# Routing the third batch one step sooner and reordering gathers and stores in a fused attention and mixture-of-experts kernel

## The chip, the cores and the metric

The kernel runs on one core of one Trainium2 chip. A core has five engines that run side by side: TensorE (PE in the profile: matmuls, with PEld for its weight loads), VectorE (DVE), ScalarE (ACT), GpSimd (POOL) and SyncE (SP). Each engine works through a queue of its own, in order, and waits on semaphores for what the others and the transfers produce. The metric is the device time of one execution in microseconds (us), the median of several runs. Lower is better.

## The reference

Two blocks follow one another. The first is a linear attention over 4 batches, 4 heads, 1088 positions and 32 channels, whose features are products of two random sketches. The second sends each of the resulting 4352 tokens of 128 channels to one of 8 experts.

```python
def phi(x):
    a = np.einsum('rd,bhsd->bhsr', S1, x)          # r = 8
    b = np.einsum('rd,bhsd->bhsr', S2, x)
    return np.einsum('bhsi,bhsj->bhsij', a, b).reshape(*x.shape[:-1], r * r)
q_p, k_p = (phi(q), phi(k))
kv = np.einsum('bhsf,bhsd->bhfd', k_p, v)
z = np.sum(k_p, axis=2)
num = np.einsum('bhsf,bhfd->bhsd', q_p, kv)
den = np.einsum('bhsf,bhf->bhs', q_p, z)[..., None] + 1e-06
attn_out = (num / den).astype(np.float32)

x = attn_out.transpose(0, 2, 1, 3).reshape(B * S, H * D)      # 4352 x 128
logits = x @ w_gate                                           # 8 experts
expert_idx = np.argmax(logits, axis=1)
gate_w = softmax(logits)[np.arange(N), expert_idx]            # (written out in the reference)
for e in range(E):
    mask = expert_idx == e
    h = np.maximum(x[mask] @ w1[e], 0.0)                      # 128 -> 1024
    out[mask] = gate_w[mask, None] * (h @ w2[e])              # 1024 -> 128
```

## The kernel before

The attention part is written as steps; the functions put at a step run in the order of a small number given with them. Tokens come out of it batch by batch. `route` handles one batch in four parts: `choose` (the best expert, on DVE), `gates` (the exponential, on ACT), `rank` (a row number for each token, from counting matmuls on PE and seven DVE operations), and `scatter` (POOL writes each group of 128 rows into an array in HBM that is sorted by expert, with one indirect DMA each).

```python
def rank():
    ...
    nc.vector.tensor_reduce(row_i, rk, AX.X, ALU.add)
    nc.vector.tensor_tensor(base_e, base_e, pr[:, ts(n, E)], ALU.add)
    ...
def scatter(us):
    for u in us:
        d = nc.gpsimd.indirect_dma_start(
            out=xs_dram[:], out_offset=bass.IndirectOffsetOnAxis(ap=row_i[:, u:u + 1], axis=0),
            in_=x[:, u, :].bitcast(I32), ...)
```

The sorted rows are then worked on in tiles of 128 rows with a single expert each. Between 34 and 41 tiles are needed, depending on how the tokens fall: tiles 0 to 33 always run (JMIN = 34, JT = 41). Tiles 34 to 40 are optional, in three parts of 4, 2 and 1 tiles, run after tiles 16, 20 and 24 if a bit of a count is set. The first ten tiles (JE = 10) hold only rows of the first two batches, so they can start while batches 3 and 4 are still being routed. For every tile, POOL gathers its rows from HBM; `x_in` transposes them on PE and copies the expert's first weights on DVE; `up` and `down` are the two matmul layers; `store` scatters the rows of the result to `out`, again with an indirect DMA of POOL.

```python
parts = [range(JMIN, JMIN + 4), range(JMIN + 4, JMIN + 6), range(JMIN + 6, JMIN + 7)]
after = {16: 0, 20: 1, 24: 2}
sequence = []
for j in range(JMIN):
    sequence += [j, *parts[after[j]]] if j in after else [j]
place = {j: p for p, j in enumerate(sequence)}
...
def gather(j):
    d = nc.gpsimd.indirect_dma_start(out=xg_bufs[place[j] % XB].bitcast(I32), ..., in_=xs_dram[:], ...)
...
def x_in(j):
    xg = xg_bufs[place[j] % XB]
    xTp = bank_ps(f"xgTp{j}")
    nc.tensor.transpose(xTp[:, :128], in_=xg[:, 0:DM], identity=ident)
    ...
def down(j):
    ...
    nc.scalar.activation(y, py[:, :DM], AF.Copy, bias=0.0, scale=xg_bufs[place[j] % XB][:, DM:DM + 1])
```

The schedule of the third batch (number 2), and the loop over the tiles:

```python
query_chunk(16, 3, 0)
query_chunk(17, 3, 1, turned=(19, 7))      # the transposes of this chunk: step 19, order 7
...
at(16, first_gathers, 0)                   # gathers of tiles 0 to 5
choose, gates, rank, scatter = route(None, 2, J)
at(18, choose, 2)
at(19, gates, 5)
at(20, rank, 6)
at(20, lambda: scatter(range(J)), 6)
at(20, lambda: x_in(0), 0)
at(20, lambda: x_in(1), 5)
at(21, lambda: up(0), 0)
...
def gather_to(p):
    nonlocal gathered
    while gathered < min(p, JT):
        gather(sequence[gathered])
        gathered += 1
...                                        # extras: the fourth batch's routing, in tiles 0 to 5
for j in range(JMIN):
    ...                                    # x_in(j + 2), up(j + 1), extras, down(j); the optional parts
    gather_to(JE if j < 5 else place[min(j + AHEAD, JMIN - 1)] + 1)      # AHEAD = 6

    if j >= 5:
        for _ in range(min(len(waiting), 2 if j + 1 < JMIN else JT)):
            store(waiting.pop(0))
```

`waiting` lists the tiles whose results are computed but not yet stored. Gathers go in the order in which tiles run, with the four optional tiles of the first part between 16 and 17, into 14 buffers in turn. Results of tiles 0 to 33 have 16 buffers in turn (`y`), those of optional tiles one each (`y_late`).

Of the kernel before, what the change touches and what calls it, by code (L numbers as in the profile page):

```python
# [35 lines left out]
I32 = mybir.dt.int32  # L36
AF = mybir.ActivationFunctionType
# [8 lines left out]
def kernel(  # L46
# [12 lines left out]
    nc = tc.nc  # L59
    B, H, S, D = q.shape  # L60
    R = S1.shape[0]
    NTOK, DM = out.shape
    E, _, F = moe_w1.shape
    NP = H // 2
    J = S // 128
# [11 lines left out]
    JT = NTOK // 128 + E - 1  # L77
    JMIN = NTOK // 128

    JE = -(-(NTOK // 2 - E * 127) // 128)  # L80
    XB = 14
    AHEAD = 6
    assert DM == H * D == 128 and H == JC == 4 and R == 8 and REM == 64 and J % JC == 0 and B % 2 == 0
    assert F == 1024 and NTOK == B * S and NTOK % 128 == 0 and E == 8
# [16 lines left out]
    def bank_ps(name):  # L101
        return ps_w.tile([128, 512], FP, tag="w", name=name)
# [108 lines left out]


    xg_bufs = []
    for i in range(XB):
        xg_bufs.append(big.tile([128, XW], FP, name=f"xg{i}"))
        nc.gpsimd.memset(xg_bufs[i], 0.0)

# [71 lines left out]
    def at(step, fn, order=1):  # L289
        steps.setdefault(step, []).append((order, len(steps.get(step, ())), fn))  # L290
# [152 lines left out]
    def rows_of(b, j, n):  # L443
        x, lgh = x_tile(b)
        return x[:, ds(j, n), 0:DM], lgh[:, ds(j, n)]

    def query_chunk(step, b, c, turned=None):
        query(f"{b}_{c}", step,
              [main["q", b][:, h, ts(c, JC), :].rearrange("p j d -> p (j d)") for h in range(H)],
              b, lambda: rows_of(b, c * JC, JC), None, turned or (step + 3, 1))  # L450
# [6 lines left out]
    xs_dram = dram.tile([E * NTOK, XW], I32, name="xs_dram")  # L457
# [193 lines left out]

    parts = [range(JMIN, JMIN + 4), range(JMIN + 4, JMIN + 6), range(JMIN + 6, JMIN + 7)]
    after = {16: 0, 20: 1, 24: 2}
    sequence = []
    for j in range(JMIN):
        sequence += [j, *parts[after[j]]] if j in after else [j]
    place = {j: p for p, j in enumerate(sequence)}
    engines = [PE, DVE, mybir.EngineType.Activation]


    def buffers(name, n, shape, dtype=FP, tags=None):
        def one(k, i):
            if tags is None:
                return big.tile(shape, dtype, name=f"{name}{k}_{i}")
            tag, bufs = tags[k]
            t = io.tile([128, H, J, DA if tag == "v_aug" else D], dtype, tag=tag, name=f"{name}{k}_{i}", bufs=bufs)
            return t.rearrange("p h j d -> p (h j d)")[:, 0:F]

        own = {}

        def of(j):
            k = int(j >= JMIN)
            if k not in own:
                own[k] = [one(k, i) for i in range(n[k])]
            return own[k][j % n[k]]

        return of

    xT_of = buffers("xgT", (3, 2), [128, 128])
    w1_of = buffers("w1", (3, 2), None, tags=(("k", 3), ("q", 3)))  # L680
    hT_of = buffers("hT", (3, 2), None, tags=(("v", 3), ("v_aug", 2)))
# [3 lines left out]
    def y_of(j):  # L685
        if j >= JMIN:
            return late_y[j - JMIN]
        if not early_y:
            for i in range(2):
                t = att.tile([128, JC * H, RR], FP, tag="q_p", name=f"y{i}").rearrange("p g f -> p (g f)")  # L690
                early_y.extend(t[:, ts(c, DM)] for c in range(8))
        return early_y[j % 16]

    def gather(j):
        d = nc.gpsimd.indirect_dma_start(  # L695
            out=xg_bufs[place[j] % XB].bitcast(I32), out_offset=None, in_=xs_dram[:],
            in_offset=bass.IndirectOffsetOnAxis(ap=tiles[j][1], axis=0),
            bounds_check=E * NTOK - 1, oob_is_err=False)
        if j < JE:
            tc.declare_no_dep(d.ins, group="late", reason="late rows are in no tile of the first group")  # L700
            tc.add_to_no_dep_group("early", d.ins)

    def x_in(j):
        xg = xg_bufs[place[j] % XB]
        xTp = bank_ps(f"xgTp{j}")
        nc.tensor.transpose(xTp[:, :128], in_=xg[:, 0:DM], identity=ident)  # L706
        xT, w1 = xT_of(j), w1_of(j)
        nc.scalar.copy(out=xT, in_=xTp[:, :128])  # L708
        _, (wo,) = nc.values_load_multi_w_load_instructions(
            tiles[j][0], engines=[DVE], min_val=0, max_val=(E - 1) * F,  # L710
            skip_runtime_bounds_check_because="the table clamps the expert to the last one")
        nc.vector.tensor_copy(out=w1, in_=w1_all[:, ds(wo, F)])  # L712

    def rows_out(j):

        to = to_of(j)
        row_id = xg_bufs[place[j] % XB][:, DM + 1:DM + 2].bitcast(I32)
        if j < JE:
            nc.vector.tensor_copy(out=to, in_=row_id)
        else:  # L720
            nc.vector.tensor_tensor(to, row_id, tiles[j][2], ALU.bitwise_or)
# [14 lines left out]
    def down(j):  # L736
        hT = hT_of(j)
        _, (wo,) = nc.values_load_multi_w_load_instructions(
            tiles[j][0], engines=[PE], min_val=0, max_val=(E - 1) * F,
            skip_runtime_bounds_check_because="the table clamps the expert to the last one")  # L740
        py = bank_ps(f"py{j}")
        for c in range(NFC):
            nc.tensor.matmul(py[:, :DM], lhsT=hT[:, ts(c, 128)], rhs=w2_all[:, ds(wo + c * DM, DM)],  # L743
                             start=(c == 0), stop=(c == NFC - 1))
        y = y_of(j)
        nc.scalar.activation(y, py[:, :DM], AF.Copy, bias=0.0, scale=xg_bufs[place[j] % XB][:, DM:DM + 1])  # L746

    def store(j):
        y = y_of(j)
# [13 lines left out]
    def run(last):  # L763
        for i in sorted(steps):
            if i <= last:
                for _, _, fn in sorted(steps.pop(i), key=lambda f: f[:2]):
                    fn()

    def first_gathers():
        for j in range(AHEAD):  # L770
            gather(j)
# [33 lines left out]
    key_end(17, 3)  # L805
    query_rem(15, 1)
    query_chunk(16, 3, 0)
    query_chunk(17, 3, 1, turned=(19, 7))
    first_table = table(0, JE, 0)
    for i in range(4):  # L810
        at(14 + i // 2, lambda: next(first_table, None), 4)
# [1 line left out]
    at(16, first_gathers, 0)  # L813
    at(18, lambda: next(first_table, None), 5)
    choose, gates, rank, scatter = route(None, 2, J)
    at(18, choose, 2)
    at(19, gates, 5)
    at(20, rank, 6)
    at(20, lambda: scatter(range(J)), 6)
    at(20, lambda: x_in(0), 0)  # L820
    at(20, lambda: x_in(1), 5)
    at(21, lambda: up(0), 0)
    run(21)

    last_table = table(1, JT - JE, JE)
# [2 lines left out]
        for _ in last_table:  # L830
            break

    gathered = AHEAD

    def gather_to(p):
        nonlocal gathered
        while gathered < min(p, JT):
            gather(sequence[gathered])
            gathered += 1

    choose, gates, rank, scatter = route(None, B - 1, J + 1)
    extras = {0: [choose, gates], 1: [rank, lambda: scatter(range(0, 2))], 2: [lambda: scatter(range(2, 5)), piece],
              3: [lambda: scatter(range(5, 7)), piece, piece], 4: [lambda: scatter(range(7, J + 1)), piece, piece, piece],
              5: [piece, piece, piece]}

    waiting = []
    for j in range(JMIN):
        here = after.get(j)
        if j + 4 == min(after):
            runs = []  # L850
            for i in range(len(parts)):
                _, (v,) = nc.values_load_multi_w_load_instructions(
                    tiles["parts"][0:1, i:i + 1], engines=engines, min_val=0, max_val=E - 1,
                    skip_runtime_bounds_check_because="bits of a number below E")
                runs.append(v)
        if here is not None:
            tiles_here = parts[here]
            rows_out(j)
            for o in tiles_here:
                rows_out(o)  # L860
            with tc.If(runs[here] > 0) as found:
                for i, o in enumerate(tiles_here):
                    if i + 1 < len(tiles_here):
                        x_in(tiles_here[i + 1])
                    else:
                        x_in(j + 2)
                    up(o)
                    down(tiles_here[i - 1] if i else j)
                up(j + 1)
                down(tiles_here[-1])  # L870
            with found.Else():
                x_in(j + 2)
                up(j + 1)
                down(j)
            waiting += [j, *tiles_here]
        else:
            if j + 2 < JMIN:
                x_in(j + 2)
            if j + 1 in after:
                x_in(parts[after[j + 1]][0])  # L880
            rows_out(j)
            if j + 1 < JMIN:
                up(j + 1)
            for fn in extras.get(j, ()):
                fn()
            down(j)
            waiting.append(j)

        gather_to(JE if j < 5 else place[min(j + AHEAD, JMIN - 1)] + 1)

        if j >= 5:
            for _ in range(min(len(waiting), 2 if j + 1 < JMIN else JT)):
                store(waiting.pop(0))


# [29 lines left out]
```

## Time and profile before

| | |
|---|---|
| time, median of 3 runs | 232.16 us (230.89 to 232.24) |
| span of the profiled execution | 230.5 us |
| PE busy | 213.0 us, 92% |
| DVE busy | 115.4 us, 50% |
| ACT busy | 76.7 us, 33% |
| POOL busy | 136.6 us, 59% |
| gathers (xg) | 41 on POOL, 1121 ns each, 2.6 us from issue to landing |
| scatters of rows (xs_dram) | 34 on POOL, 1029 ns each, 2.4 us to landing |
| stores (out_dram) | 34 and 7 on POOL, the 34 at 1047 ns each, 2.3 us to landing |

Times of one execution count from the start of the span. Every group of instructions is told with its engine, its source line (L706 is line 706), what it writes and reads, how often it ran, and the idle time of its engine just before, with what ended it. For the indirect DMAs on POOL the duration is that of the instruction; when the data has landed is told separately. L706 is the transpose in `x_in`, L727 and L743 are the matmuls of `up` and `down`, L519 the scatter of routed rows, L695 the gather, L746 the result (y) and L750 its store.

### The profile page before, as it was taken

The numbers are of one execution on the slowest core, as the hardware profiler recorded it, in microseconds if no ns is written. First come the engines' busy times: TensorE is split into PE (matmuls) and PEld (weight loads), VectorE is DVE, ScalarE is ACT, GpSimd is POOL, SyncE is SP. The second block draws the span as 40 slices with busy tenths as digits, with TensorE's granted clock in tenths as the row PEclk, the third lists the DMA queues.
The fourth block names the chain that finished last, engine by engine and source line by source line (L and its number), as shares of the span: only waits on it lengthen the run. The fifth ranks groups of instructions, "written<-read, shape, count | busy, mean of one in ns | idle before, by whom it ended". The sixth has DMA issues, their size and how long they took to land.

```text
span 230.5 us, 5436 instructions
## 1 busy us (share of the span) xinstructions
PE 213.0 (92%) x1858; PEld 208.7 (91%) x1858; DVE 115.4 (50%) x339; ACT 76.7 (33%) x206; POOL 136.6 (59%) x178
## 2 busy tenths in 40 slices
PE   8799999999996999999499995899999999999992
PEld 8699999999884999999499995899999999999992
DVE  5447478987878688852224243043532433243320
ACT  2424535434434234343113331122322333222230
POOL 3365001277758377776677777777777871762313
PEclk9999999999999999999889999799999999999999
DMA  5899999981111111111011211111111110110000
GB/s 178 192 324 352 342 332 355 340 273 47 49 46 38 35 40 57 46 49 58 25 43 49 57 41 32 40 49 50 47 32 44 50 41 27 33 40 20 14 23 15
DMA packets 22988, 22.61 MB, mean 98 GB/s; under 512 B 5828, under 2 KB 20168, under 8 KB 22960
## 3 DMA queue, kind: packets, MB, share of 16 engines
q1 hardware_dynamic: 19232, 15.08, 22.0%
q0 software_dynamic: 3712, 7.15, 10.5%
q8 instruction: 18, 0.29, 0.5%
q14 instruction: 10, 0.08, 0.1%
q10 hardware_dynamic: 16, 0.00, 0.0%
HBM read 17.81 MB, written 4.95 MB: 99 GB/s over the span
## 4 chain that ended last, share of the span: by engine, by line
PE 67%; issue 10%; DMA 7%; POOL 6%; DVE 4%; ACT 3%; POOLq 1%; DVEq 0%; ACTq 0%
PE ph L727 21%; PE py L743 19%; PE kv L330 7%; PE nd L410 5%; DMA xg<-xs_dram,grow 5%; POOL xs_dram L519 4%; PE ab_q L308 3%; PE ab_k L308 3%; PE qp L395 2%; PE idle L151 2%; DMA xs_dram<-x_rows,row_i 2%; PE xgTp L706 2%; ACT q_pT L398 1%; POOL out_dram L750 1%; PE tp_k L301 1%
## 5 line engine op out<-in xcount | busy, mean ns | idle before, releaser
L727 PE MATMUL ph<-xgT,w 128*128 128x128 f32 x592 | 75.2, 283 | 0.0
L743 PE MATMUL py<-w_all,hT 128*128 x592 | 72.2, 276 | 0.2 <-issue 0.2
L727 PEld LDWEIGHTS ph<-xgT,w 128*128 128x128 f32 x592 | 71.9, 199 | 0.0
L743 PEld LDWEIGHTS py<-w_all,hT 128*128 128x128 f32 x592 | 69.1, 192 | 0.4 <-issue 0.4
L734 DVE TENSOR_SCALAR hT<-ph 128x512 f32<-128x512 f32 x30 | 20.8, 692 | 80.0 <-ACT hT L729 80.0
L695 POOL DMA_INDIRECT xg<-xs_dram,grow x41 | 46.0, 1121 | 16.3 <-issue 9.2
L750 POOL DMA_INDIRECT out_dram<-y,to x34 | 35.6, 1047 | 28.2 <-ACT xgT L708 11.6
L519 POOL DMA_INDIRECT xs_dram<-x_rows,row_i x34 | 35.0, 1029 | 18.4 <-issue 8.8
L729 ACT ACTIVATE hT<-ph 128x512 f32<-128x512 f32 x37 | 22.1, 597 | 55.5 <-PE ph L727 54.1
L712 DVE COPY w<-w_all 128x1024 f32 x38 | 26.2, 695 | 3.8 <-issue 2.1
L746 ACT ACTIVATE y<-py,xg 128x128 f32<-128x128 f32 x34 | 12.5, 367 | 36.2 <-PE py L743 35.1
L410 PE MATMUL nd<-kvx,q_pT 128*128 128x82 f32 x128 | 15.8, 276 | 1.9 <-ACT q_pT L398 1.9
L410 PEld LDWEIGHTS nd<-kvx,q_pT 128*128 128x128 f32 x128 | 14.9, 192 | 2.6 <-ACT q_pT L398 2.6
L182 POOL COPY v_aug<-v 128x1024 f32<-128x1024 f32 x4 | 4.2, 1042 | 20.8 <-DMA v<-in_v_dram 20.8
L706 PE MATMUL xgTp<-ident,xg 128*128 128x128 f32 x38 | 10.3, 283 | 6.3 <-DMA xg<-xs_dram,grow 6.3
L330 PE MATMUL kv<-v_aug,k_p 128*128 128x66 f32 x128 | 15.4, 273 | 0.0
L330 PEld LDWEIGHTS kv<-v_aug,k_p 128*128 128x128 f32 x128 | 14.9, 193 | 0.1
L708 ACT COPY xgT<-xgTp 128x128 f32<-128x128 f32 x38 | 9.7, 260 | 10.1 <-PE xgTp L706 9.1
L398 ACT COPY q_pT<-qp 128x512 f32<-128x512 f32 x16 | 8.6, 589 | 11.8 <-PE qp L395 11.8
L706 PEld LDWEIGHTS xgTp<-ident,xg 128*128 128x128 f32 x38 | 5.5, 147 | 6.7 <-issue 6.6
L317 DVE TENSOR_TENSOR k_p<-sum_k 128x1024 f32<-128x1024 f32 x8 | 9.8, 1225 | 0.3
L317 DVE TENSOR_TENSOR q_p<-sum_q 128x1024 f32<-128x1024 f32 x8 | 9.8, 1225 | 0.3
(172 smaller groups left out, 204.6 us busy)
## 6 DMA issues: line engine op xcount, KB each, us to landing
w_all<-in_moe_w_dram SPq DMA_DIRECT2D x16, 512.0 KB, 8.7
k<-in_k_dram SPq DMA_DIRECT2D x4, 512.0 KB, 5.1
v<-in_v_dram SPq DMA_DIRECT2D x4, 512.0 KB, 5.2
q<-in_q_dram SPq DMA_DIRECT2D x4, 512.0 KB, 7.8
xg<-xs_dram,grow POOLq DMA_INDIRECT x41, 2.6
xs_dram<-x_rows,row_i POOLq DMA_INDIRECT x34, 2.4
out_dram<-y,to POOLq DMA_INDIRECT x34, 2.3
k_rem<-in_k_dram SPq DMA_DIRECT2D x4, 32.0 KB, 4.4
```

The source lines that it names most:

```text
L317: nc.vector.tensor_tensor(dst.rearrange("p g (a b) -> p g a b", a=R), s[:, :, 0:R, None].broadcast_to([128, n * 4, R, R]), s[:, :, None, R ...
L330: nc.tensor.matmul(kv[b][:, ts(hp, 2 * DA)], lhsT=lhs[:, ts(hp, 128)], rhs=rhs[:, ts(hp, 2), :], start=(first and hp == 0), stop=last, ski ...
L410: nc.tensor.matmul(o, lhsT=lhsT, rhs=kvx[b][:, hp].rearrange("p g c -> p (g c)"), start=True, stop=True)
L519: d = nc.gpsimd.indirect_dma_start(out=xs_dram[:], out_offset=bass.IndirectOffsetOnAxis(ap=row_i[:, u:u + 1], axis=0), in_=x[:, u, :].bitc ...
L695: d = nc.gpsimd.indirect_dma_start(out=xg_bufs[place[j] % XB].bitcast(I32), out_offset=None, in_=xs_dram[:], in_offset=bass.IndirectOffset ...
L706: nc.tensor.transpose(xTp[:, :128], in_=xg[:, 0:DM], identity=ident)
L712: nc.vector.tensor_copy(out=w1, in_=w1_all[:, ds(wo, F)])
L727: nc.tensor.matmul(ph[:, ts(c, 128)], lhsT=w1[:, ts(c, 128)], rhs=xT, start=True, stop=True)
L729: nc.scalar.activation(hT[:, 0:512], ph[:, 0:512], AF.Relu)
L734: nc.vector.tensor_scalar(hT[:, 512:1024], ph[:, 512:1024], 0.0, None, ALU.max)
L743: nc.tensor.matmul(py[:, :DM], lhsT=hT[:, ts(c, 128)], rhs=w2_all[:, ds(wo + c * DM, DM)], start=(c == 0), stop=(c == NFC - 1))
L750: d = nc.gpsimd.indirect_dma_start(out=out[:], out_offset=bass.IndirectOffsetOnAxis(ap=to_of(j), axis=0), in_=y, in_offset=None, bounds_ch ...
```

## The change

Three things are altered together. The third batch is routed one step sooner: its choice moves from step 18 to 17, its exponential from 19 to 18, its ranking and scatters from 20 to 19, so that POOL can write its rows sooner. The optional tiles get seven gather buffers of their own, beside 11 for the others, and their gathers are spread, one a tile from tile 7 on, instead of standing in the queue where the tiles run. And the stores of results start later: none before tile 7, one in every second tile while optional gathers remain, then two a tile; so that gathers come first in POOL's queue.

```diff
-    XB = 14
+    XB = 11
...
-    for i in range(XB):
+    for i in range(XB + JT - JMIN):
         xg_bufs.append(big.tile([128, XW], FP, name=f"xg{i}"))
         nc.gpsimd.memset(xg_bufs[i], 0.0)
...
-    sequence = []
-    for j in range(JMIN):
-        sequence += [j, *parts[after[j]]] if j in after else [j]
-    place = {j: p for p, j in enumerate(sequence)}
...
+    def xg_of(j):
+        return xg_bufs[j % XB if j < JMIN else XB + j - JMIN]
...          (each xg_bufs[place[j] % XB] becomes xg_of(j))
-    query_chunk(17, 3, 1, turned=(19, 7))
+    query_chunk(17, 3, 1, turned=(19, 5))
...
-    at(18, choose, 2)
-    at(19, gates, 5)
-    at(20, rank, 6)
-    at(20, lambda: scatter(range(J)), 6)
+    at(17, choose, 2)
+    at(18, gates, 5)
+    at(19, rank, 7)
+    at(19, lambda: scatter(range(J)), 8)
...          (gather_to goes away)
-    waiting = []
+    waiting, optional = [], list(range(JMIN, JT))
...
-        gather_to(JE if j < 5 else place[min(j + AHEAD, JMIN - 1)] + 1)
-
-        if j >= 5:
-            for _ in range(min(len(waiting), 2 if j + 1 < JMIN else JT)):
+        for i in range(AHEAD, JE) if j == 0 else range(JE, j + AHEAD + 1) if j == 5 else [j + AHEAD] if j > 5 else []:
+            if i < JMIN:
+                gather(i)
+        if j > 6 and optional:
+            gather(optional.pop(0))
+        for _ in range(0 if j < 6 else j % 2 if optional else 2 if j + 1 < JMIN else JT):
+            if waiting:
                 store(waiting.pop(0))
```

## The prediction

> **What bounds the kernel now.** I read the page first, then the chain of waits, then PE's timeline, and last POOL's timeline, because each answer named the next question.
>
> The engine table of the page and its clock row:
>
> ```profile
> PE 213.0 (92%) x1858; PEld 208.7 (91%) x1858; DVE 115.4 (50%) x339; ACT 76.7 (33%) x206; POOL 136.6 (59%) x178
> PEclk9999999999999999999889999799999999999999
> ```
>
> PE is busy nearly all the time, so only its holes and its slow stretches can give time back. The clock row shows where: of its 40 slices of 5.76 us the 20th and 21st (109 to 121 us) and the 26th (144 to 150 us) are below 9. PE's timeline around the two (start, duration, engine, line, tiles, count, idle before and what ended it):
>
> ```profile
> 108.94 1.95 PE L743 MATMUL py<-w_all,hT 128*128 x16
> 113.77 0.31 PE L706 MATMUL xgTp<-ident,xg 128*128 128x128 f32 x1 [2.88 <-DMA xg<-xs_dram,grow]
> ...
> 139.48 1.95 PE L743 MATMUL py<-w_all,hT 128*128 x16
> 144.86 0.73 PE L706 MATMUL xgTp<-ident,xg 128*128 128x128 f32 x2 [3.43 <-DMA xg<-xs_dram,grow]
> ```
>
> Both times the transpose of a token tile waits for the gather of its rows. Counting transposes (one a tile), the first is tile 10, the second tile 17. The busy time by stretches shows the second cost; the columns are the stretch, its length, then PE, PEld, DVE, ACT and POOL busy, the granted clock, DMA share and GB/s:
>
> ```profile
> 103.47:107.15 3.68, 3.68 (x35) 3.68 (x34) 0.93 (x2) 1.12 (x3) 2.90 (x3) 1.00 0.16 54
> 113.77:117.39 3.62, 3.62 (x18) 3.62 (x19) 0.00 (x0) 0.27 (x1) 3.01 (x3) 0.53 0.20 60
> 144.86:148.62 3.76, 3.76 (x20) 3.66 (x21) 0.00 (x0) 0.53 (x2) 2.97 (x3) 0.57 0.16 44
> ```
>
> An undisturbed tile takes 3.68 us and 35 matmuls. After each hole the same 3.7 us hold only 18 or 20, at a clock of 0.53 or 0.57: a hole costs its length and then some 1.7 us of slow work.
>
> Why the gathers are late stands in the chain of waits (start, duration, what):
>
> ```profile
> 106.06 0.97 POOL xs_dram L519
> 107.03 0.30 issue
> 107.33 2.36 DMA xs_dram<-x_rows,row_i
> 109.82 0.52 issue
> 110.55 3.08 DMA xg<-xs_dram,grow
> 113.77 0.31 PE xgTp L706
> ...
> 136.04 2.46 DMA xg<-xs_dram,grow
> 138.54 0.49 issue
> 139.17 2.43 DMA xg<-xs_dram,grow
> ```
>
> Before the first hole POOL is issuing the fourth batch's row scatters one after another, and the gather of tile 10 waits for the last one to land. Before the second hole the chain is gathers alone. POOL's own timeline says where its queue lost time:
>
> ```profile
> 76.76 0.99 POOL L695 DMA_INDIRECT xg<-xs_dram,grow  x1 [0.30 <-issue]
> 80.79 1.03 POOL L519 DMA_INDIRECT xs_dram<-x_rows,row_i  x1 [3.04 <-DVE base_e L513]
> 82.13 1.16 POOL L519 DMA_INDIRECT xs_dram<-x_rows,row_i  x1 [0.30 <-issue]
> ```
>
> After the sixth gather POOL idles 3.04 us until DVE has ranked the third batch; from there to 110.55 it never idles more than a step of 0.30 us, apart from the landing wait. So POOL's queue, started at 80.79, sets when tile 10 may begin.
>
> [...] The trace has 0.53 and 0.57 after 2.88 and 3.43 us[...]; gaps of 1.16 us (at 72.79) and 1.11 us (at 75.10) left 1.00. [...] The trace has 2.36 us for that scatter, 3.08 for that gather and a median of 2.6 for gathers. [...] hence the 2.17 us ahead of 110.55, which the change keeps.
>
> **The change part by part.**
>
> *Third batch earlier.* The order of instructions shows no instruction added or removed on PE, DVE or ACT, only moves: six DVE operations of the choice go ahead of the last query chunk's sum and product, the exponential ahead of one ACT copy, the ranking matmuls ahead of tile 0's transpose, and DVE's seven rank operations ahead of tile 0's weight copy. I lay these out with durations of the DVE timeline. The choice takes 1.8 us (lgs at 71.59 to the next operation at 73.39) and can start at 69.27, when the product before it is issued, where DVE idled 0.64 us; so the last chunk's sum moves from 69.99 to 71.07. The exponential holds the ACT copy of the gate block to 70.6 (from 69.86), which delays PE's remainder rows and both query transposes by 0.72 us: the second from 72.79 to 73.51. The ranking matmuls follow at 74.4, about 0.3 us. The numerator matmuls, at 75.10 before, waited for ACT to copy the second query transpose; in the new order they wait on DVE, which is done at 74.2, and can start at 74.9. So PE loses nothing here; I count 0. The row numbers are ready near 75.7 instead of 80.5, ahead of POOL's sixth gather, which is issued until 77.75. POOL then goes on at 78.05 instead of 80.79: **2.74 us earlier**, and all its following work, which had no other wait, moves along. The fourth batch's ranks were done at 87.7 and its scatters move from 96.73 to 93.99, so nothing there turns into a wait.
>
> Tile 10's transpose goes from 113.77 to 111.03. PE would be free at 107.04 + 3.68 = 110.72, so a hole of 0.3 to 0.7 us stays, under the 1.16 that cost no clock. Tile 11 then starts at 111.03 + 3.68 = 114.71, not 119.17: **4.46 us**, of which 2.74 is wait and 1.72 is clock.
>
> *Gathers of the optional tiles.* Before, POOL's order from gather 10 had gather 17 in place 22 (counting from 0), because eleven stores, six gathers and the gathers of tiles 34 to 37 stood between. In the new order it is in place 13: the same ten gathers but only two stores stand between. POOL's pace: 57 steps from 110.55 to 190.01, so 1.394 us a step. Gather 17 is issued at 107.81 + 13 x 1.394 = 125.9 and lands 2.6 later, 128.5. PE needs it at 111.03 + 7 x 3.68 = 136.8. The hole goes, with 8 us to spare. Its price before: transpose 16 at 137.58 to transpose 18 at 150.25 is 12.67 us; without it two tiles and one extra transpose, 7.36 + 0.11 = 7.47. **5.20 us.** That part 0 (tiles 34 to 37) isn't run shows in y_late: 3 results, of parts 1 and 2; its gathers are issued all the same.
>
> *Stores put off.* POOL has the same 72 gathers and stores left after gather 10. It runs them from 107.81; from tile 14 on there are three a tile, 4.18 us against PE's 3.68, so it falls behind PE's place in the program, but three optional tiles give PE 11 us more. The last gather, tile 33, is in place 61: 192.8, landed 195.4; PE needs it at 216.97 - 9.66 = 207.3. After it come ten stores; POOL has caught up by tile 29, and the end (last y, store, landing) is as before. Buffers: result 33 takes the place of store 17, in place 47, near 173; not close. The four added memsets are 4 x 0.21 = 0.83 us near 16 us, where POOL later waits 13.8 us for v. Nothing.
>
> Sum: 4.46 + 5.20 = 9.66; 232.16 - 9.66 = **222.5**.
>
> **The rivals.** (a) *A hole at tile 10 stays long enough to slow the clock.* If row numbers come later than I lay out, or POOL's steps are slower (one gather took 1.98 us, another 1.55), the hole grows by that much[...]: 225 to 226. Against it: 2 us of spare between 75.7 and 77.75. (b) *POOL becomes the bound.* With stores put off, POOL has no idle time up to the last tiles; were a step 1.6 us, the last gather would land at 208 and its store queue end late, some 224 to 227. Against it: the pace before was measured with the same mix. (c) *The routed chain was hidden anyway, and the moved DVE and ACT work delays PE at 70 to 77 us.* PE's order has slack only up to tile 10, where POOL decides; a delay of up to 0.3 us is swallowed. It would make 222.5 to 223.5. (d) *Only the optional part acts:* 232.16 - 5.20 = 227.
>
> **Range and chances.** Both gains rest on the two largest idle rows of PE. Little lies below: without any hole at tile 10 it is 0.3 us less, and the three runs of before spread by 1.35. Above, (a) and (c) weigh most: 221.0 to 225.2. Faster by over 2% means under 227.5; only (d) or a POOL much slower than its pace reaches it: 0.94. Within 2% 0.04, slower 0.02.
>
> **What would show it.** Right: the first scatter of the third batch follows the sixth gather by 0.30 us, near 78; transpose 10 near 111 with less than 1 us idle before it and a clock of 1.00 after; no idle row at transpose 17; POOL without waits until some 195; chain of waits mostly PE. Wrong: 18 to 20 matmuls in the 3.7 us after a hole; waits of transposes on gathers after tile 14; ACT's y or DVE's row copy waiting for a store; a last store long after the last y.

## The result and the profile after

The changed kernel takes **223.8 us** (median of four runs, 223.25 to 225.9) against 232.2 us before (230.89 to 232.24): a ratio of 0.9666 with a 95% interval of 0.9605 to 0.9726. The prediction had 222.5, from 221.0 to 225.2. The profiled execution is the longest of the four, 225.9 us with a span of 224.1; its mean granted clock was 0.975, that of the others 0.989 to 0.996.

The page after, its engine table, its clock row and its chain of waits by engine:

```profile
PE 213.5 (95%) x1858; PEld 210.0 (94%) x1858; DVE 115.8 (52%) x339; ACT 76.3 (34%) x206; POOL 138.1 (62%) x182
PEclk9999999999999559999999999999999999999999
PE 86%; DVE 5%; issue 4%; ACT 2%; POOL 1%; POOLq 1%; ACTq 0%; DVEq 0%
```

The weak slices of before, at 109 to 121 and at 144 to 150 us, are full. The chain holds no transfer any more and is nearly all PE. But there are two new slices at 5: with 5.6 us each, they are 73 to 84 us, a place where before had none.

POOL's timeline after (start, duration, line, tiles, count, idle before and what ended it): the sixth gather, the third batch's first scatter, the gathers of tiles 10, 17 and 33, and the first store behind them.

```profile
76.61 1.00 POOL L694 DMA_INDIRECT xg<-xs_dram,grow  x1 [0.30 <-issue]
77.91 1.39 POOL L519 DMA_INDIRECT xs_dram<-x_rows,row_i  x1 [0.30 <-issue]
...
108.13 1.05 POOL L694 DMA_INDIRECT xg<-xs_dram,grow  x1 [2.18 <-DMA xs_dram<-x_rows,row_i]
...
125.77 1.26 POOL L694 DMA_INDIRECT xg<-xs_dram,grow  x1 [0.30 <-DMA xg<-xs_dram,grow]
...
192.97 1.04 POOL L694 DMA_INDIRECT xg<-xs_dram,grow  x1 [0.31 <-DVE to L720]
200.36 0.97 POOL L749 DMA_INDIRECT out_dram<-y,to  x1 [2.00 <-ACT xgT L707]
```

Where before lost 3.04 us ahead of the third batch's scatters, 0.30 are left. The gather of tile 17, in place 13 from that of tile 10, is issued at 125.77. Before, it was in place 22 and was issued at 142.08; the two transfers at 136.04 and 139.17 that the prediction's chain shows belong to the optional tiles 34 and 36, which stood ahead of it. POOL's line of before:

```profile
142.08 1.05 POOL L695 DMA_INDIRECT xg<-xs_dram,grow  x1 [0.30 <-issue]
```

After the landing wait that ends at 108.13, the changed kernel's POOL waits for nothing of note until 200.36.

PE's timeline after, from the front of the routing to tile 17:

```profile
70.89 0.50 PE L415 MATMUL nd_r<-kvx,q_pT_r 128*64 128x82 f32 x6 [0.82 <-ACT kvx L374]
71.32 1.09 PE L395 MATMUL qp<-ident,q_p 128*128 128x128 f32 x8
73.57 1.97 PE L395 MATMUL qp<-ident,q_p 128*128 128x128 f32 x8 [1.16 <-DVE done L646]
75.96 3.55 PE L410 MATMUL nd<-kvx,q_pT 128*128 128x82 f32 x16
...
114.71 0.27 PE L705 MATMUL xgTp<-ident,xg 128*128 128x128 f32 x1
...
140.49 0.38 PE L705 MATMUL xgTp<-ident,xg 128*128 128x128 f32 x2
```

Tile 10's transpose (114.71) and tile 17's (140.49, with the next tile's beside it) have no idle time ahead of them: both holes are gone. Yet tile 10 starts later than the 111.03 that POOL would have allowed, and indeed later than the 113.77 of before. The reason is in the rows from 73.57 on: eight query transposes took 1.09 us at 71.32, and the next eight 1.97 at 73.57. The stretches say it directly (stretch, length, then PE, PEld, DVE, ACT and POOL busy, granted clock, DMA share, GB/s):

```profile
68.48:73.57 5.09, 3.11 (x26) 2.57 (x26) 4.78 (x14) 2.17 (x7) 3.78 (x3) 0.96 0.10 26
73.57:82.92 9.35, 9.35 (x51) 9.28 (x52) 4.55 (x18) 1.51 (x4) 7.22 (x8) 0.50 0.18 53
```

For 9.35 us PE ran at a granted clock of 0.50, though no gap ahead of it was longer than 1.16 us.

**Where the 8 us lie.** PE is the bound, so the start of two transposes, tile 11 and tile 18, cuts the span into three parts. Part of the differences in the first piece is not the kernel's. The program opens with 24 matmuls of zeros, and their time changes from profile to profile. In the kernel before (a row of the chain of waits, then one of PE's timeline):

```profile
1.06 4.67 PE idle L151 x24
```

```profile
68.39 1.16 PE L308 MATMUL ab_q<-s_cat,xT_q 128*128 128x128 f32 x8 [0.40 <-ACT xT_q L303]
```

The second row, the last feature matmuls ahead of the moved work, is taken as a mark. The same changed program had the zeros at 4.75 us and the mark at 68.48 in the first profile, and the mark at 69.08 in its second one (g2). So tile 11 is given from the mark too. All numbers are from PE's timelines (us); the kernels a to h2 are those of the experiments.

| kernel | mark | tile 11 starts | from mark to tile 11 | tile 11 to 18 | tile 18 to the end of the span |
|---|---|---|---|---|---|
| before | 68.39 | 119.17 | 50.78 | 31.08 | 80.3 |
| as predicted | 68.39 | 114.71 | 46.32 | 25.88 | 80.3 |
| changed, first profile | 68.48 | 118.39 | 49.91 | 25.89 | 79.8 |
| changed, another chip (g2) | 69.08 | 116.26 | 47.18 | 25.88 | 80.0 |
| routing alone (a) | 69.14 | 116.31 | 47.17 | 31.63 | 79.9 |
| queue alone (b) | 69.56 | 120.32 | 50.76 | 25.88 | 80.5 |
| stores as before (c) | 68.99 | 116.17 | 47.18 | 31.50 | 80.8 |
| optional gathers in run order (d) | 69.46 | 116.74 | 47.28 | 25.88 | 79.8 |
| rank behind tile 0's operands (h2) | 68.48 | 114.85 | 46.37 | 25.88 | 80.6 |

The end is the same everywhere within 1 us. The second gain is 5.20 us and, within 0.01, identical wherever it appears. The way from the mark to tile 11 is where the kernels with the sooner routing differ, and where the prediction was off: only h2 has what it drew.

### The profile page after: what moved, and what is told of

It is laid out like the page before. It is cut to its first block, busy times and chain, and to the rows that moved or that the text cites. A ratio compares the mean times of both kernels' runs of the same rounds, so it can differ in the third digit from the quotient of the medians.

```text
span 224.1 us, 5429 instructions
## 1 busy us (share of the span) xinstructions
PE 213.5 (95%) x1858; PEld 210.0 (94%) x1858; DVE 115.8 (52%) x339; ACT 76.3 (34%) x206; POOL 138.1 (62%) x182
## 4 chain that ended last, share of the span: by engine, by line
PE 86%; DVE 5%; issue 4%; ACT 2%; POOL 1%; POOLq 1%; ACTq 0%; DVEq 0%
PE ph L726 29%; PE py L742 27%; PE kv L330 7%; PE nd L410 7%; PE ab_k L308 3%; PE ab_q L308 3%; PE qp L395 2%; PE idle L151 2%; PE xgTp L705 2%; DVE q_p L317 2%; POOL out_dram L749 1%; PE tp_k L301 1%; PE tp_q L301 1%; ACT q_pT L398 1%; DVE k_p L317 1%
## 5 line engine op out<-in xcount | busy, mean ns | idle before, releaser
L726 PE MATMUL ph<-xgT,w 128*128 128x128 f32 x592 | 73.8, 279 | 0.0
L726 PEld LDWEIGHTS ph<-xgT,w 128*128 128x128 f32 x592 | 70.7, 196 | 0.0
L694 POOL DMA_INDIRECT xg<-xs_dram,grow x41 | 44.7, 1091 | 16.3 <-issue 7.3
L749 POOL DMA_INDIRECT out_dram<-y,to x34 | 36.6, 1076 | 24.5 <-ACT xgT L707 10.4
L410 PE MATMUL nd<-kvx,q_pT 128*128 128x82 f32 x128 | 17.5, 296 | 0.8 <-ACT q_pT L398 0.8
L410 PEld LDWEIGHTS nd<-kvx,q_pT 128*128 128x128 f32 x128 | 16.9, 213 | 1.3 <-ACT q_pT L398 1.3
L182 POOL COPY v_aug<-v 128x1024 f32<-128x1024 f32 x4 | 4.8, 1200 | 17.2 <-DMA v<-in_v_dram 17.2
L395 PE MATMUL qp<-ident,q_p 128*128 128x128 f32 x64 | 9.3, 293 | 1.2 <-DVE done L646 1.2
```

What stands on the lines that cost most here:

```text
L410: nc.tensor.matmul(o, lhsT=lhsT, rhs=kvx[b][:, hp].rearrange("p g c -> p (g c)"), start=True, stop=True)
L694: d = nc.gpsimd.indirect_dma_start(out=xg_of(j).bitcast(I32), out_offset=None, in_=xs_dram[:], in_offset=bass.IndirectOffsetOnAxis(ap=tile ...
L726: nc.tensor.matmul(ph[:, ts(c, 128)], lhsT=w1[:, ts(c, 128)], rhs=xT, start=True, stop=True)
L749: d = nc.gpsimd.indirect_dma_start(out=out[:], out_offset=bass.IndirectOffsetOnAxis(ap=to_of(j), axis=0), in_=y, in_offset=None, bounds_ch ...
```

## The experiments

The theory: each hole of PE is set by one place in POOL's queue. The third batch's scatters set when tile 10's gather is issued, and the stores ahead of tile 17's gather set that of tile 17. Rivals: the whole gain comes from the queue, the routing was hidden anyway; or what gains is the private buffers and the spreading of the optional gathers rather than the stores put off.

**a. Only the third batch's moves**, in the kernel before:

```diff
-    query_chunk(17, 3, 1, turned=(19, 7))
+    query_chunk(17, 3, 1, turned=(19, 5))
-    at(18, choose, 2)
-    at(19, gates, 5)
-    at(20, rank, 6)
-    at(20, lambda: scatter(range(J)), 6)
+    at(17, choose, 2)
+    at(18, gates, 5)
+    at(19, rank, 7)
+    at(19, lambda: scatter(range(J)), 8)
```

> The third batch is routed one step sooner, gathers and stores stay as before. Theory (POOL's place in the queue decides each hole): the gather of tile 10 is issued 2.4 to 2.7 us sooner, near 108, and the hole of 2.88 us at tile 10 is gone or under 1 us; but gather 17 is still 22 places behind it, so it lands only 2.4 to 2.7 us sooner, near 142, and whatever PE gained beyond that turns into a hole at tile 17. The whole gain is POOL's 2.4 to 2.7 us, or up to 4.3 if the hole at 17 becomes too short to slow the clock: 228 to 230 us. Rival (the two gains are independent and add): tile 10's 4.5 us come through in full, 227.7 us, with a hole at tile 17 of 3.4 us as before.

Measured: 229.67 us (229.01 to 230.19), ratio 0.9889 [0.9847, 0.9932]. PE's timeline at tile 17, and the stretch after it:

```profile
142.60 0.66 PE L706 MATMUL xgTp<-ident,xg 128*128 128x128 f32 x2 [4.02 <-DMA xg<-xs_dram,grow]
```

```profile
142.60:146.30 3.70, 3.70 (x20) 3.70 (x21) 0.00 (x0) 0.48 (x2) 3.06 (x3) 0.57 0.15 41
```

The hole at tile 10 is gone (tile 11 starts 2.86 us sooner), but the hole at tile 17 grew from 3.43 to 4.02 us and is still followed by a clock of 0.57: PE arrives 2.86 us sooner, and the transpose behind the gather starts only 2.26 sooner (142.60 against 144.86). So the routing is not hidden, but alone it is worth 2.2 us by the medians of that chip (231.84 before), since part of it turns into the next wait.

**b. Only gathers and stores**: the changed kernel with the routing put back (the edit of a in reverse).

> Gathers and stores as changed, the third batch routed as before. Theory: the hole of 2.9 us at tile 10 with its slow clock stays (gather 10 issued near 110.5), the hole at tile 17 is gone, 5.2 us less: 227.0 us. No slow stretch of PE between 73 and 83 us, if that stretch in the changed kernel comes from the moved choice and exponential. Rival (the slow stretch is a matter of the run, or of something the gathers and buffers changed): it can turn up here as well.

Measured: 227.12 us (226.49 to 228.51), ratio 0.9771 [0.973, 0.9813]. PE's timeline at tiles 10 and 17, and the stretch after the first:

```profile
114.92 0.30 PE L705 MATMUL xgTp<-ident,xg 128*128 128x128 f32 x1 [2.86 <-DMA xg<-xs_dram,grow]
...
142.41 0.38 PE L705 MATMUL xgTp<-ident,xg 128*128 128x128 f32 x2
```

```profile
114.92:118.62 3.70, 3.70 (x23) 3.70 (x24) 0.29 (x1) 0.86 (x2) 2.98 (x3) 0.69 0.18 48
```

The mirror of a: the hole at tile 10 as before (2.86 us, clock 0.69 after it), none at tile 17. Each part takes away its own hole. Alone they bring 2.2 and 4.7 us by the medians, 6.9 in sum, and together 7.9 (g2 below, 223.75 against 231.69, on another chip; d below, on the chip of a and b, has 7.6).

**c. The changed kernel with the stores as before**, two in every tile from tile 5 on; own buffers and spread gathers stay:

```diff
-        for _ in range(0 if j < 6 else j % 2 if optional else 2 if j + 1 < JMIN else JT):
+        for _ in range(0 if j < 5 else 2 if j + 1 < JMIN else JT):
```

> The changed kernel, but stores two a tile from tile 5 on as before, so that the optional gathers are spread and have their own buffers, and the stores are not put off. Theory (the stores put off are what brings gather 17 forward): gather 17 stands again some 22 places behind gather 10, is issued near 108.1 + 22 x 1.39 = 138.7 and lands near 141.4; a hole at tile 17 of up to 4.6 us: 226 to 229 us. Rival (own buffers and spreading are what counts): no hole at tile 17, 223.8 us as the changed kernel.

Measured: 229.78 us (228.35 to 230.31), ratio 0.9874 [0.9826, 0.9923], above what was expected. PE's timeline at tiles 15 and 16, and the stretch after:

```profile
132.56 0.30 PE L705 MATMUL xgTp<-ident,xg 128*128 128x128 f32 x1 [1.09 <-DMA xg<-xs_dram,grow]
138.45 0.30 PE L705 MATMUL xgTp<-ident,xg 128*128 128x128 f32 x1 [1.95 <-DMA xg<-xs_dram,grow]
```

```profile
138.40:142.00 3.60, 3.55 (x18) 3.56 (x19) 0.00 (x0) 0.27 (x1) 2.91 (x3) 0.58 0.12 37
```

The waits did not vanish, they moved: with an optional gather and two stores beside each gather POOL has four instructions a tile, at the 1.394 us a step of the prediction 5.6 us against PE's 3.68, and falls behind already at tiles 15 and 16. The place was misjudged in the expectation (tile 17), not the kind. Its time equals that of a: without the stores put off, spreading and own buffers bring nothing.

**d. The changed kernel with the optional gathers where their tiles run**, the stores put off as in the changed kernel:

```diff
-        if j > 6 and optional:
-            gather(optional.pop(0))
-        for _ in range(0 if j < 6 else j % 2 if optional else 2 if j + 1 < JMIN else JT):
+            for o in parts[after[i]] if i in after else ():
+                gather(o)                              # (within the loop over the gathers)
+        for _ in range(0 if j < 6 else j % 2 if j < 13 else 2 if j + 1 < JMIN else JT):
```

> The changed kernel, but the gathers of the optional tiles stand in a block where their part runs (four between the gathers of 16 and 17, as before), still in buffers of their own; stores put off as in the change. Theory (stores decide): gather 17 is at about the same place 13, no hole at tile 17, 223.8 us, the same as the changed kernel within 0.5. Rival (spreading counts): a hole at tile 17 comes back, 226 or more.

Measured: 224.22 us (223.24 to 225.85), ratio 0.9665 [0.9603, 0.9726]: the changed kernel's time. The spreading is worth nothing that can be measured; the stores put off are the second gain. Whether 14 buffers in turn would have served as well was not tried. PE's timeline at tile 10 and the page's clock row:

```profile
112.97 0.30 PE L705 MATMUL xgTp<-ident,xg 128*128 128x128 f32 x1 [0.81 <-DMA xg<-xs_dram,grow]
113.10 2.01 PE L726 MATMUL ph<-xgT,w 128*128 128x128 f32 x16
```

```profile
PEclk9999999999999999999999999999999999999999
```

Here PE kept its clock at 73 us, came to tile 10 ahead of POOL, and waited 0.81 us: the kind of small hole that the prediction had drawn. No loss of clock shows behind it: the 16 matmuls took 2.01 us, against 1.95 in the tile after it, and the clock row stays at 9. But it came later than drawn, and tile 11 is 47.28 us behind the mark, no sooner than in a, c and g2, which lost clock at 73 us (0.66, 0.65 and 0.60 from 73.50 to 75.50). POOL's first gather, first scatter and gather of tile 10, and the stretch that ends ahead of the second query transposes:

```profile
71.47 1.04 POOL L694 DMA_INDIRECT xg<-xs_dram,grow  x1 [2.19 <-DVE sh L476]
80.24 1.08 POOL L519 DMA_INDIRECT xs_dram<-x_rows,row_i  x1 [0.30 <-issue]
110.28 1.05 POOL L694 DMA_INDIRECT xg<-xs_dram,grow  x1 [2.18 <-DMA xs_dram<-x_rows,row_i]
```

```profile
69.46:74.56 5.10, 3.11 (x27) 2.58 (x27) 4.79 (x14) 2.17 (x7) 2.78 (x2) 1.00 0.09 26
```

The gather of tile 10 is issued 40.82 us behind the mark, against 39.42 predicted. POOL was late before the moved work: its first gather stands 2.01 us behind the mark, 0.80 in the kernel before. And PE was as sparsely busy, 3.11 of 5.10 us, as in the changed kernel's first profile, yet kept a clock of 1.00.

**The slow stretch at 73 us.** It is the one thing in the profile after that the prediction had not. Two questions: is it there in other executions, and does the moved work cause it? That sparse work of PE, or a gap in it, lowers the clock there is the author's conjecture, from the first profile: 3.11 us busy of 5.09, with gaps of 0.82 and 1.16 us, ahead of a clock of 0.50. The changed kernel was run again, on another chip (g2), beside a variant (h2) that leaves the choice and the exponential where they were and puts only the ranking and the scatters sooner, behind tile 0's transpose and weight copy:

```diff
-    query_chunk(17, 3, 1, turned=(19, 5))
+    query_chunk(17, 3, 1, turned=(19, 7))
-    at(17, choose, 2)
-    at(18, gates, 5)
-    at(19, rank, 7)
-    at(19, lambda: scatter(range(J)), 8)
+    at(18, choose, 2)
+    at(19, gates, 5)
...
     at(20, lambda: x_in(0), 0)
+    at(20, rank, 0)
+    at(20, lambda: scatter(range(J)), 0)
```

> The changed kernel unaltered, once more, because on the chip of the earlier look at it every kernel took some 282 us, the one before too. 223.8 us. Theory (sparse work of PE at 69 to 73.6 halves the clock for a length that changes from run to run): a slow stretch of some length begins near 73.6, or none; where it is short, tile 10 shows a hole of 0.3 to 0.8 us on its gather. Rival (an accident of the first profile): no slow stretch and a mean clock of 0.995 or more in all its runs.

> Gathers and stores as changed; the third batch's choice and exponential where they were before, only its ranking and scatters moved forward, behind tile 0's transpose and weight copy. Theory: the row numbers are ready near 77.6, POOL goes on near 78; PE's gaps at 70 to 75 are no longer than before and the ranking matmuls fill part of one, so the clock stays at 1.00 there; a hole of 0.3 to 0.8 us at tile 10, none at tile 17: 222.5 us, about 1 us below the changed kernel. Rival (the slow stretch comes with any sooner routing, or with the run): 223.8 us and a mean clock under 0.99 in some runs.

Measured: g2 223.75 us (223.52 to 223.95), ratio 0.9656 [0.9617, 0.9695]; h2 **222.91 us** (222.71 to 223.19), ratio 0.9622 [0.9582, 0.9661]. All four runs of h2 lie below all four of g2, so h2 is the fastest version found, by 0.84 us. PE's timeline and stretches of g2:

```profile
71.48 0.50 PE L415 MATMUL nd_r<-kvx,q_pT_r 128*64 128x82 f32 x6 [0.81 <-ACT kvx L374]
74.17 1.97 PE L395 MATMUL qp<-ident,q_p 128*128 128x128 f32 x8 [1.16 <-DVE done L646]
...
112.57 0.27 PE L705 MATMUL xgTp<-ident,xg 128*128 128x128 f32 x1
```

```profile
73.50:75.50 2.00, 1.33 (x6) 1.34 (x7) 1.66 (x11) 0.61 (x2) 1.70 (x2) 0.60 0.17 42
75.50:79.50 4.00, 3.79 (x33) 3.56 (x33) 1.86 (x8) 1.51 (x4) 3.08 (x4) 0.77 0.22 50
79.50:83.00 3.50, 3.50 (x34) 3.50 (x34) 1.50 (x5) 1.08 (x2) 2.58 (x4) 1.00 0.12 40
```

The same two gaps, and the same slow stretch, but it ends before 79.50 where it lasted until 82.9 in the first profile. Tile 2's transpose is at 82.76 instead of 84.90 (80.91 before). Now PE, POOL and the stretches of h2:

```profile
72.88 1.09 PE L395 MATMUL qp<-ident,q_p 128*128 128x128 f32 x8 [1.16 <-ACT q_pT L398]
75.19 2.01 PE L410 MATMUL nd<-kvx,q_pT 128*128 128x82 f32 x16 [0.89 <-ACT q_pT L398]
...
111.13 0.27 PE L705 MATMUL xgTp<-ident,xg 128*128 128x128 f32 x1
```

```profile
78.33 1.02 POOL L519 DMA_INDIRECT xs_dram<-x_rows,row_i  x1 [0.31 <-DVE den L422]
```

```profile
68.48:72.88 4.40, 3.11 (x27) 2.58 (x27) 3.62 (x7) 1.98 (x7) 2.04 (x2) 1.00 0.10 30
72.88:75.19 2.31, 1.42 (x18) 1.31 (x19) 2.07 (x11) 1.33 (x4) 1.77 (x2) 1.00 0.24 63
```

In h2 the eight transposes take 1.09 us, the clock stays at 1.00, and the scatters still follow the sixth gather by 0.31 us. Tile 10 starts at 111.13, without a hole: 0.10 from the predicted 111.03. Moving the choice and the exponential was not needed for the gain; moving the ranking was.

What a slow stretch costs can be read from all runs, since each has its mean granted clock. The profiles give the scale: 0.975 with the long stretch (first profile), 0.989 with the short one (g2), 0.999 with none (d).

| mean clock of the run | times (us) |
|---|---|
| 0.975 | 225.90 (changed, first), 225.85 (d) |
| 0.989 to 0.990 | 223.79, 223.81 (changed, first), 223.60, 223.89 (g2) |
| 0.995 to 1.000 | 223.25 (changed, first), 223.52, 223.95 (g2), 223.24, 224.21, 224.22 (d) |
| 0.997 to 0.999, h2 | 222.71, 222.79, 223.03, 223.19 |

The long stretch costs some 2.1 us. The short one costs nothing that these runs show: the second row has a mean of 223.77, the third of 223.73. In d's profile, where the clock is kept, PE waits for the gather of tile 10 instead. So the kept clock does not explain why h2 is the fastest: it is below the runs of the third row as well. In its profile none of the six gathers ahead of the scatters takes over 1.04 us, where d has one of 1.90 and g2 one of 1.73; one profile of each does not show that this is the reason.

**What triggers the slow stretch** was to be told apart by two further variants of the changed kernel: one with idle matmuls put into the two gaps, one with the exponential behind the ACT copy that PE waits for.

```diff
+    at(19, filler(7), 0)      # f: seven and nine matmuls of zeros, result not used
+    at(19, filler(9), 2)
```

```diff
-    at(18, gates, 5)          # i
+    at(19, gates, 0)
```

They ran twice, on one chip, the first time beside the changed kernel (g) and the variant h.

> The changed kernel with 16 matmuls of zeros more, 7 in PE's gap of 0.82 us at 70 and 9 in that of 1.16 us at 72.5. Theory (the clock is halved because PE's work at 69 to 73.6 is sparse): no slow stretch from 73.5 on, mean clock at 0.995 or more in all runs, tile 2 near 81.5, a hole of up to 0.8 us at tile 10: 222.7 to 223.2 us, below the changed kernel's 223.8. Rival (zeros don't count as work for the clock, or the gaps aren't the cause): slow stretches as in the changed kernel, 223.8 us or more.

> The changed kernel with the exponential behind the ACT copy of the gate block, which then no longer waits for DVE's choice. Theory (the exponential's place makes the gap of 0.82 us, and this gap makes the difference to the clock): the remainder matmuls run on with a gap of 0.1 us, the gap ahead of the second query transpose stays at 1.2 to 1.3, no slow stretch, tile 2 near 81.2: 222.7 to 223.2 us. Rival (DVE's choice ahead of the last chunk's sum is a cause by itself): slow stretches as in the changed kernel, 223.8 us.

Measured: f 288.57 us, ratio 1.0262 [1.0191, 1.0334], then 288.53, ratio 1.012 [1.002, 1.0221]; i 281.8, ratio 1.0019 [0.9941, 1.0096], then 282.76; g 282.18, ratio 1.0008 [0.9908, 1.0108]; h 282.91, ratio 1.0057 [0.9978, 1.0136]. On that chip the kernel before took 281.97 and 284.01 us too, with a mean clock of 0.87 to 0.92 in its runs, against 0.98 to 0.99 on the others, so these times say nothing of the stretch at 73 us. The waits and POOL's timeline of g show in part why (engine and line, waited for: us in all, times, longest):

```profile
PEld py L742 <- issue: 16.5, 26, 1.7
PE py L742 <- issue: 12.2, 21, 1.2
```

```profile
92.62 1.02 POOL L519 DMA_INDIRECT xs_dram<-x_rows,row_i  x1 [11.04 <-DVE base_e L513]
```

PE pauses between its own matmuls without a wait that the profile shows, and POOL waits 11.04 us for the ranks: with PE that late, POOL's queue has slack, which fits that its order is worth nothing here (282.18 against 281.97). In i's profile the gap ahead of the remainder rows is gone, as meant; whether the clock would then stay at 1.00 on a chip like the others is not shown. Nor does f separate anything: it lies 6.4 us above g.

So the trigger stays open, and the conjecture is not shown. What stands is an association: on the chips where before took some 232 us, the slow stretch is in four of five profiles of kernels with the choice and exponential moved (the changed kernel twice, a and c, not d), and in none of three without (before, b, h2). By the mean clocks it is in 6 of the 12 runs of the changed kernel and d tabled above, and in none of the four of h2. That is too little to rule out chance in h2, and what differs between executions of one program is not known.

## Why the prediction was right

**Third batch earlier: right.** The first scatter at 77.91 (predicted 78.05), 0.30 us behind the sixth gather, so the row numbers were there in time; tile 10's gather was issued at 108.13 (107.81).

**Tile 17: right in place and size.** Its gather was issued at 125.77 (125.9). The stretch from tile 11 to tile 18 fell by 5.19 or 5.20 us in every kernel that has the stores put off and not in the others; predicted 5.20.

**Stores put off: right.** The last gather at 192.97 (192.8), the first wait behind it at 200.36, and the end unchanged: last y to end of span 4.3 us before and after.

**What was mis-sized: the first term, "4.46 us, of which 2.74 is wait and 1.72 is clock".** Counted from the mark it came to 0.87 us in the first profile, 3.60 in g2, 3.50 in d, and 4.41 in h2. Two things took from it, and the profiles show them one at a time.

In the first profile and in g2 it is PE's clock. "So PE loses nothing here; I count 0" laid out delays of single instructions, and these came as laid out (the second query transposes start at 73.57, predicted 73.51), but from there on the clock fell, to 0.50 for 9.35 us in the one and to 0.60 and then 0.77 over 6.0 us in the other: tile 2 is 3.90 and 1.16 us later behind the mark than before. PE so late finds the gather of tile 10 already there, so the predicted small hole is missing. In d, where the clock held (1.00 from 69.46 to 79.00), the count of 0 is nearly right (tile 2 is 0.20 us later), but "POOL then goes on at 78.05" is not: that is 9.66 us behind the mark, and d has 10.78. PE then waits for tile 10's gather, and its transpose comes 4.66 us after that of tile 9, not 3.68.

In h2, where neither happens, tile 18 starts at 140.73, against 150.25 - 9.66 = 140.59. Its time of 222.91 is 8.78 us below that of before on the same chip, 231.69. So the path was right, and the number inside the range, but 1.3 us of the stated 222.5 were missed; with both faults seen in some profiles and neither in all runs, how the 1.3 us divides among them stays open. The clock alone is not the answer: at 0.995 and above the changed kernel still took 223.25 to 223.95.

**The rivals.** (c), moved DVE and ACT work delaying PE at 70 to 77 us, named the place, but 223.8 and 223.75 lie above its 222.5 to 223.5, and what PE lost there was clock, in about half of the runs, not a delay of 0.3 us. (a), a hole at tile 10 long enough to slow the clock, did not come: there is no hole in the first profile and g2, and behind that of 0.81 in d the 16 matmuls took 2.01 us, where those behind the first hole of before took 3.64 us at a clock of 0.53. (b) did not come. (d) is what b measured, 227.12 against 227, and the changed kernel is 3.3 us below it.

For what a hole does to the clock, before had shown 0.53 and 0.57 after 2.88 and 3.43 us, and 1.00 after gaps of 1.16 and 1.11 us. The stretch as a whole was not weighed when a delay of 0.72 us was added to it: in before PE was busy 3.11 of its 4.40 us (68.39 to 72.79), at 1.00. The first profile has 3.11 of 5.09 and then 0.50 for 9.35 us; d, with 3.11 of 5.10 and then 1.00, shows that the busy share alone does not decide it.

## What to carry to other kernels

When a busy engine has a few holes, trace each to the in-order queue that feeds it, and move out of that queue's way whatever nobody waits for yet: here the stores put off were worth 5.2 us, and the spreading of the gathers nothing that could be measured. Removing one hole alone can hand part of the gain to the next (2.2 and 4.7 us alone, 7.9 together), so look at the next wait before sizing the first. And when a stage runs PE sparsely, try first to move only the link of the chain that the queue waits for, and leave alone the DVE and ACT queues that PE hangs on: h2 does so and was 0.84 us faster, though the runs do not show through what. Before profiles are compared, a mark ahead of the change takes out what differs from run to run: here up to 1.2 us, nearly as much as the miss that was to be explained.

## What the runs showed of the hardware

A granted clock of 0.50 for 9.35 us came after gaps of no more than 1.16 us, with PE busy 3.11 of 5.09 us (first profile). The same program had a shorter slow stretch in another profile (g2, over before 79.5). After the same gaps, busy 3.11 of 5.10 us, d stayed at 1.00, and so did h2 with 3.11 of 4.40; the busy share of these 5 us does not settle it. A hole of 2.86 us brought a clock of 0.69 (b), and one of 1.95 us, 5.9 us behind one of 1.09, brought 0.58 (c), where the hole of 1.09 itself left 1.00 for the next 3.7 us and a lone one of 0.81 (d) left 16 matmuls at 2.01 us. What else decides the clock is not settled by these runs.

The 24 matmuls of zeros at the start took 4.67 us in before and 4.75 in the first profile, and the mark came 1.17 us later in b (69.56) than before. Nor is it known why one chip ran at a mean clock of about 0.9 and paused PE between its own matmuls, 12.2 us in all on one line (g), where the first profile has no such wait of note on that line.
